# A fourth buffer for the q, k and v of a banded attention, and loads handed over six blocks ahead from the 16th block on

## The chip, the cores and the metric

The kernel runs on one core of a Trainium2 chip. The time is the device time of one execution in microseconds; less is better. The engines are TensorE (PE), VectorE (DVE), ScalarE (ACT), GpSimd (POOL) and SyncE (SP), which here only issues DMA transfers. Each engine works through a queue of its own in a fixed order and waits on semaphores for the others.

## What is computed

Three parts follow one another. The first is an attention in which each row sees itself and the 63 rows before it. The second adds the real part of a two-dimensional Fourier transform, and then an MLP on the normalised sum. The third is a gated MLP, whose mixing of rows is a product with a 576 by 576 matrix.

```
B, H, S, D = 4, 8, 576, 64                       # q, k, v
rel = pos[:, None] - pos[None, :]
scores = where((rel >= 0) & (rel < 64), q @ k.T / sqrt(D), -1e9)
x = softmax(scores) @ v                           # -> [B, S, 512]

mixed = real(fft(fft(x, axis=1), axis=2))
u = x + mixed
un = (u - mean(u)) / sqrt(var(u) + 1e-6)
x = u + maximum(un @ w_ch1, 0) @ w_ch2            # 512 -> 2048 -> 512

h = gelu(x @ w_in)                                # 512 -> 1024, in halves u, v
v = (v - mean(v)) / sqrt(var(v) + 1e-6) * g_ln
out = x + (u * (w_sg @ v + b_sg)) @ w_out
```

All is in float32. Where precision asks for it a number is split into a high and a low half, and one product becomes three matmuls (`mm3`, L130 to L132).

## The kernel before

**Attention.** The 4 x 9 = 36 blocks n have 64 query rows each. `scores` (L328) multiplies q by k for the eight heads, two heads at a time, into one of two PSUM tiles `sc`. VectorE adds the mask and finds the row's extreme (L333, results `s` and `mx`), and ScalarE takes the exponential (L335). One block later TensorE transposes the result into `pt` (L342), ScalarE copies it to `pts` (L344). Two blocks later, for two blocks at once, TensorE multiplies by v into the tile `pv` (L355), of which there is one in PSUM; VectorE normalises from there (L370 `rc`, L371 `rd`, L374 `x`). Three blocks later `x` is transposed (L384 `xt`) and copied to `uT` (L386), and VectorE folds it for the transform (L464 `E`, L465 `O`, L469, L470 `F`). In the last batch that is one fold over the whole batch, 128 x 1152, inside `dft`.

**Loads of attention.** All go over SP's queue. `load_q` fills one of `QB` tiles of a ring for two blocks, `load_k` one of three tiles for three blocks, `load_v` one of `VB` tiles for two blocks, with a lag of `VL` = 2 blocks. The loop hands over the loads of block n + 4 after the scores of block n. A load into a used tile waits until the last reader of the tile is done: `sc` for q and k, `pv` for v.

**What runs beside it.** `dft(b)` (L506 to L568) is the transform of batch b: first products with `eh` and `oh`, the halves of E and F, against a table (256 or 258 columns), then products with `ah`, `bh` against a second table (290 columns); VectorE adds the results into `uT` (L559 to L562). `ln(n)` is the layer norm of chunk n of 384 rows: transposes L637, statistics on VectorE (L641 BN_STATS, L642, L618 to L622, and `nb` at L648), ScalarE applies them (L650), then transposes L656 and copies L659, L661 into `xh` or `xhm`. LN(0) is the norm of the first chunk, LN(1) of the second. `raw` and `halves` decode weights: after a load `dec_s` three steps L166 (VectorE), L165 (ScalarE), L167 (VectorE) make a number, and L171 (ScalarE), L172 (VectorE in the MLP) split it into the tile `set`. In `mlp` TensorE makes `h` from `xh` and a set, ScalarE takes `rh` (L717), VectorE `rl` (L718), and TensorE multiplies these into four `acc` tiles; after the fourth set VectorE adds `acc` to `uT` (L703).

**What sets the order.** The parts are generators. A scheduler takes from them by their estimated times and priorities, and it fixes the order of every engine's queue when the kernel is built. The order of the instructions is nowhere written out: a wait that the estimate sees in one place moves what stands behind it on all engines. PSUM and SBUF tiles come from pools, and a tile of a pool is free for the next user when its last reader is done.

Of the kernel before, what the change touches and what calls it, by code (L numbers as in the profile page):

```python
# [11 lines left out]
F32 = mybir.dt.float32  # L12
# [33 lines left out]
LAG, XPT = (1, 2, 3), 0  # L46
STRETCH = (1.6, 1.0)
FP = ()
UB, SB, QB, VB = 4, 3, 3, 3
WARM, W0, W1 = 16, 9000, 2500  # L50
TAB_AT = (2, 4, 7, 9)
D45 = 3000
# [61 lines left out]
class Kernel:  # L114
# [152 lines left out]
        self.kt, self.vt = {}, {}  # L267

    def load_k(self, b, g):
        t = self.ap_.tile([128, 4, 256], F32, tag="k", bufs=3, name="k")  # L270
        o = 192 * g
        for c in (slice(0, 128), slice(128, 256)) if b == g == 0 else (slice(0, 256),):
            self.nc.sync.dma_start(t[:, :, c], self.aps["k"][b, :, :, o + c.start:o + c.stop])
            if b == g == c.start == 0:
                self.nc.scalar.dma_start(self.mask, self.aps["mask"])
        self.kt[b, g] = t
# [40 lines left out]
    def attention(self):  # L317
# [4 lines left out]
        def scores(n):  # L322
            b, j = divmod(n, NB)
            q, k = self.qt.pop((b, j)), self.kt[b, j // 3]
            sc = ps.tile([128, 4, 128], F32, tag="sc", bufs=2, name="sc")
            for hp in range(4):
                o = 64 * (j % 3)
                nc.tensor.matmul(sc[:, hp], lhsT=q[:, hp].rearrange("p a b -> p (a b)"), rhs=k[:, hp, o:o + 128], start=True, stop=True)  # L328
            mx = p.tile([128, 4], F32, tag="mx", bufs=3, name="mx")
            s = p.tile([128, 4, 128], F32, tag="s", bufs=SB, name="s")  # L330
            mask = self.mask[:, int(j == 0)]
            for hp in range(4):
                nc.vector.tensor_tensor_reduce(out=s[:, hp], in0=sc[:, hp], in1=mask, scale=-0.125, scalar=1e30, op0=ALU.add, op1=ALU.min, accum_out=mx[:, hp:hp + 1])  # L333
            for hp in range(4):
                nc.scalar.activation(out=s[:, hp], in_=s[:, hp], func=AF.Exp, bias=mx[:, hp:hp + 1], scale=-1.0)  # L335
            st[n], st['mx'] = s, mx

        def transposes(n):
            pr = st.pop(n)
            pt = ps.tile([128, 4, 128], F32, tag="pt", bufs=1 + XPT, name="pt")  # L340
            for hp in range(4):
                nc.tensor.transpose(pt[:, hp], pr[:, hp], self.ident)  # L342
            pts = p.tile([128, 4, 128], F32, tag="pts", bufs=3, name="pts")
            nc.scalar.activation(out=pts, in_=pt, func=AF.Copy)  # L344
            st[n] = pts

        def pv(n):

            b, j = divmod(n, NB)
            both = [n - 1, n] if j % 2 else [n]  # L350
            ops = [(64 * (m % NB % 2), st.pop(m), self.vt.pop((b, m % NB))) for m in both]
            st["pv"] = o = ps.tile([128, 2, 512], F32, tag="pv", name="pv")
            for i in range(8):
                for r, pts, v in ops:
                    nc.tensor.matmul(o[r:r + 64, i // 4, 65 * (i % 4):65 * (i % 4) + 65],  # L355
                                     lhsT=pts[:, i // 2, 64 * (i % 2):64 * (i % 2) + 64],
                                     rhs=v[:, 65 * i:65 * i + 65], start=True, stop=True)

        def norm(n):
            o = st["pv"]  # L360
            m = 64 if n % NB == NB - 1 else 128
            ov = o[:m, :, 0:260]
            if NV:
                y = p.tile([128, 2, 260], F32, tag="y", bufs=2, name="y")
                nc.scalar.activation(out=y[:m], in_=ov, func=AF.Copy)
                ov = y[:m]
            ov = ov.rearrange("p a (h e) -> p a h e", e=65)
            rc = p.tile([128, 2, 4, 1], F32, tag="rc", bufs=2, name="rc")
            rd = p.tile([128, 2, 4, 1], F32, tag="rd", bufs=2, name="rd")
            nc.vector.tensor_scalar(out=rc[:m], in0=ov[:, :, :, 64:65], scalar1=1e-9, scalar2=None, op0=ALU.add)  # L370
            nc.vector.reciprocal(out=rd[:m], in_=rc[:m])  # L371
            x = p.tile([128, 514], F32, tag="x", bufs=2, name="x")
            xv = x[:m].rearrange("p (a c) -> p a c", a=2)[:, :, 0:256].rearrange("p a (h e) -> p a h e", e=64)
            (nc.gpsimd if NV == 2 else nc.vector).tensor_tensor(out=xv, in0=ov[:, :, :, 0:64], in1=rd[:m].to_broadcast([m, 2, 4, 64]), op=ALU.mult)  # L374
            nc.gpsimd.tensor_scalar(out=x[:m, 256:257], in0=x[:m, 512:513], scalar1=1.0, scalar2=None, op0=ALU.mult)
            st["x", n] = x

        def xt(n):
            b, j = divmod(n, NB)
            m, x = 64 if j == NB - 1 else 128, st.pop(("x", n))  # L380
            i = j // 2
            t = ps.tile([128, 4, 128], F32, tag="pt", bufs=2, name="xt") if XPT else ps.tile([128, 4, 128], F32, tag="xt", name="xt")
            for c in range(4):
                nc.tensor.transpose(t[:, c, 0:m], x[:m, 128 * c:128 * c + 128], self.ident[:m, :m])  # L384
            t0 = S * b + 128 * i
            nc.scalar.activation(out=self.uT[:, :, t0:t0 + m], in_=t[:, :, 0:m], func=AF.Copy)  # L386
            self.folds(b, i, t)
            if j == NB - 1:
                self.xdone = b
# [8 lines left out]
        for n in range(N + LAG[2] + 1):  # L398
            if n in TAB_AT:
                tab_at = TAB_AT.index(n)  # L400
            else:
                tab_at = None
            if n < N:
                scores(n)
            if tab_at is not None:
                self.load_tables(tab_at, st["mx"])
            self.load_attn(n + 4)
            if n < N:
                yield 870
            m = n - LAG[0]  # L410
            if 0 <= m < N:
                transposes(m)
                yield 440
            m = n - LAG[1]
            if 0 <= m < N and full(m):
                pv(m)
                yield 1800 if m % NB % 2 else 900
                norm(m)
            m = n - LAG[2]
            if 0 <= m < N and full(m):  # L420
                xt(m)
                yield 440
# [1113 lines left out]
```

## Time and profile before

| | |
|---|---|
| median of 3 runs | 766.68 us (765.56 to 767.56) |
| the profiled execution | 765.43 us |
| its span, first to last instruction | 763.6 us |
| mean granted TensorE clock | 0.998 of full speed |
| PE busy | 746.0 us, 98% of the span |
| DVE busy | 526.7 us, 69% |
| ACT busy | 350.9 us, 46% |
| POOL busy | 192.6 us, 25% |
| bytes moved | 123.37 MB |

Busy is the time in which an engine works on an instruction. The profiled execution is one of several; the terms of a sum come from it, and its own time is to be held against the sum.

### The profile page before, as it was taken

What the parts mean: (1) busy time and instruction counts of PE and PEld (TensorE: products, weight loads), DVE (VectorE), ACT (ScalarE), POOL (GpSimd) and SP (SyncE); (2) the same over time, 40 slices, a digit from 0 to 9 for tenths busy, and PEclk for the clock granted to TensorE, in tenths of its full rate; (3) what the DMA queues carried; (4) which work ended last, traced back from release to release, by engine and by line L of the source; (5) the groups of instructions that cost most, each with busy time, mean ns of one, the idle gap of its engine ahead of it and who ended that gap; (6) DMA issues with size and microseconds to landing.
All of it is one profiled execution on the core that took longest, in us unless ns stands there. A gap on an engine that the chain in (4) does not pass through costs nothing.

```text
span 763.6 us, 13934 instructions
## 1 busy us (share of the span) xinstructions
PE 746.0 (98%) x4994; PEld 720.1 (94%) x4994; DVE 526.7 (69%) x1482; ACT 350.9 (46%) x837; POOL 192.6 (25%) x244
## 2 busy tenths in 40 slices
PE   7999899899999999999999999999999999999998
PEld 6798798899999999999999999999999898999897
DVE  4768857983446599874588658546987679674662
ACT  5896996745144566331245224124646454231220
POOL 2344464434214450065321112021102211010100
PEclk9999999999999999999999999999999999999999
DMA  9998761433016888584838914753111141114023
GB/s 267 320 298 258 202 209 43 140 110 125 1 30 215 281 262 292 190 330 161 319 118 318 355 59 151 289 207 124 57 58 32 40 132 33 63 32 135 11 73 124
DMA packets 84773, 123.37 MB, mean 162 GB/s; under 512 B 24416, under 2 KB 61664, under 8 KB 84704
## 3 DMA queue, kind: packets, MB, share of 16 engines
q1 hardware_dynamic: 82912, 119.13, 47.0%
q0 software_dynamic: 576, 2.97, 1.0%
q8 instruction: 39, 0.64, 0.3%
q10 hardware_dynamic: 1216, 0.39, 0.2%
q14 instruction: 30, 0.25, 0.1%
HBM read 91.79 MB, written 30.67 MB: 160 GB/s over the span
## 4 chain that ended last, share of the span: by engine, by line
PE 77%; DVE 3%; DMA 1%; issue 1%; ACT 0%; ACTq 0%
PE w L130 7%; PE w L132 7%; PE w L131 7%; PE c L132 6%; PE c L131 6%; PE c L130 6%; PE g L130 6%; PE g L132 6%; PE g L131 5%; PE acc L131 3%; PE acc L132 3%; PE h L130 3%; PE h L131 3%; PE h L132 3%; PE acc L130 3%; DMA dec_s<-in_wo 1%
## 5 line engine op out<-in xcount | busy, mean ns | idle before, releaser
L171 ACT ACTIVATE set<-dec_w 128x256 fp32r<-128x256 f32 x111 | 45.0, 414 | 68.8 <-PE w L131 31.1
L846 POOL TENSOR_TENSOR u<-u 128x384 f32<-128x384 f32 x15 | 18.6, 1243 | 184.8 <-ACT u L845 126.4
L619 POOL TENSOR_TENSOR rq<-rq,mhalf 128x1 f32<-128x1 f32 (+1 forms) x24 | 16.0, 665 | 150.8 <-DVE rq L618 149.7
L335 ACT ACTIVATE s<-s,mx 128x128 f32<-128x128 f32 x144 | 47.5, 393 | 13.3 <-DVE mx L333 13.2
L172 DVE TENSOR_TENSOR set<-dec_w,set 128x256 fp32r<-128x256 f32 x99 | 45.4, 467 | 9.7 <-ACT set L171 3.6
L333 DVE CUSTOM_DVE_ANT_0 s<-sc,mask 128x128 f32<-128x128 f32 x144 | 33.3, 284 | 24.7 <-PE sc L328 13.2
L165 ACT ACTIVATE dec_g<-dec_s 128x256 f32<-128x256 f32 x88 | 37.5, 428 | 27.4 <-DMA dec_s<-in_wi 11.5
L132 PE MATMUL acc<-rh,set 128*128 128x384 f32 x144 | 48.6, 338 | 0.0
L131 PE MATMUL acc<-rl,set 128*128 128x384 f32 x144 | 48.5, 337 | 0.0
L130 PE MATMUL acc<-rh,set 128*128 128x384 f32 x144 | 46.7, 337 | 0.0
L167 DVE SCALAR_TENSOR_TENSOR dec_w<-dec_g,dec_w 128x256 int32<-128x256 int32 x88 | 42.0, 480 | 3.2 <-ACT dec_g L165 2.9
L328 PE MATMUL sc<-k,q 128*128 128x128 f32 x288 | 40.2, 287 | 3.2 <-DVE mx L333 1.8
L846 DVE TENSOR_TENSOR u<-w,u 128x384 f32<-128x384 f32 x44 | 24.3, 552 | 27.4 <-POOL u L846 22.6
L328 PEld LDWEIGHTS sc<-k,q 128*128 128x128 f32 x288 | 35.8, 197 | 5.1 <-issue 1.8
L893 DVE TENSOR_TENSOR uT<-g,uT 128x384 f32<-128x384 f32 x36 | 19.3, 553 | 28.1 <-PE g L132 28.1
L130 PE MATMUL c<-set,set 128*128 128x320 f32 (+2 forms) x120 | 36.2, 303 | 0.0
L132 PE MATMUL c<-set,set 128*128 128x320 f32 (+2 forms) x120 | 36.0, 303 | 0.0
L718 DVE SCALAR_TENSOR_TENSOR rl<-h,rh 128x384 fp32r<-128x384 f32 x36 | 19.8, 551 | 23.3 <-ACT rh L717 23.3
L131 PE MATMUL c<-set,set 128*128 128x320 f32 (+2 forms) x117 | 35.1, 302 | 0.0
L166 DVE TENSOR_SCALAR dec_w<-dec_s 128x256 int32<-128x256 int32 x88 | 31.0, 361 | 5.0 <-DMA dec_s<-in_wo 3.5
L355 PEld LDWEIGHTS pv<-v,pts 128*64 128x64 f32 x576 | 23.3, 139 | 8.0 <-issue 6.4
L845 ACT ACTIVATE u<-w 128x384 f32<-128x384 f32 x29 | 14.1, 487 | 35.9 <-PE w L132 35.0
(383 smaller groups left out, 2603.2 us busy)
## 6 DMA issues: line engine op xcount, KB each, us to landing
dec_s<-in_w SPq DMA_DIRECT2D x64, 256.0 KB, 3.2
v<-in_v SPq DMA_DIRECT2D x16, 520.0 KB, 5.1
xht<-xb SPq DMA_DIRECT2D x10, 768.0 KB, 8.3
xhm<-xb SPq DMA_DIRECT2D x10, 768.0 KB, 7.6
xlm<-xb SPq DMA_DIRECT2D x8, 768.0 KB, 8.2
k<-in_k SPq DMA_DIRECT2D x11, 512.0 KB, 6.3
xf<-u SPq DMA_DIRECT2D x18, 256.0 KB, 3.1
p<-xf SPq DMA_DIRECT2D x24, 192.0 KB, 3.8
```

Of the source, the lines that this page charges most:

```text
L130: mm(out, lhsT=lh, rhs=rh, start=first and i == 0, stop=False)
L131: mm(out, lhsT=lh, rhs=rl, start=False, stop=False)
L132: mm(out, lhsT=ll, rhs=rh, start=False, stop=last and i == n - 1)
L165: nc.scalar.activation(out=g, in_=s[:, :, 1].bitcast(F32), func=AF.Prelu, scale=2.0 ** -112, alpha=-2.0 ** 32)
L166: nc.vector.tensor_scalar(out=w, in0=s[:, :, 0], scalar1=29, scalar2=None, op0=ALU.logical_shift_right)
L167: nc.vector.scalar_tensor_tensor(out=w, in0=g[:].bitcast(I32), scalar=3, in1=w, op0=ALU.logical_shift_left, op1=ALU.bitwise_or)
L171: self.nc.scalar.activation(out=hi, in_=f, func=AF.Copy)
L172: self.low.tensor_tensor(out=lo, in0=f, in1=hi, op=ALU.subtract)
L328: nc.tensor.matmul(sc[:, hp], lhsT=q[:, hp].rearrange("p a b -> p (a b)"), rhs=k[:, hp, o:o + 128], start=True, stop=True)
L333: nc.vector.tensor_tensor_reduce(out=s[:, hp], in0=sc[:, hp], in1=mask, scale=-0.125, scalar=1e30, op0=ALU.add, op1=ALU.min, accum_out=mx[ ...
L335: nc.scalar.activation(out=s[:, hp], in_=s[:, hp], func=AF.Exp, bias=mx[:, hp:hp + 1], scale=-1.0)
L846: add = lambda eng, o, i, j: eng.tensor_tensor(out=o, in0=i, in1=j, op=ALU.add)
```

## The change

The ring of q gets a fourth tile, and so do the pools of k and v. The loop hands over the loads of block n + 4 for the first 16 blocks, at block 16 those of blocks 20, 21 and 22 together, and from then on those of block n + 6.

```diff
-UB, SB, QB, VB = 4, 3, 3, 3
+UB, SB, QB, VB, KB = 4, 3, 4, 4, 4
+FAR = 16
...
-        t = self.ap_.tile([128, 4, 256], F32, tag="k", bufs=3, name="k")
+        t = self.ap_.tile([128, 4, 256], F32, tag="k", bufs=KB, name="k")
...
-            self.load_attn(n + 4)
+            for m in {True: (n + 4,), n == FAR: (n + 4, n + 5, n + 6), n > FAR: (n + 6,)}[True]:
+                self.load_attn(m)
```

The number of matmuls and of transfers stays as it is. Two memsets each come to VectorE and GpSimd for the fourth q tile (L264, L265). Since the scheduler sees other loads, the order on all engines is another one from about the ninth block on, until some 200 us; behind that the same instructions follow in the same order, but for the numbers of some tiles. In the changed text all lines behind the new one are one further down, and behind the new loop two, so that L641 of before is L643, L656 is L658, and L166 is L167.

VectorE at the statistics of LN(0), among the blocks of attention. Before, two BN_STATS (L641) and a decode step (L166) stand around `rc`, and a second decode step stands right ahead of `x` some rows further down:

```order
L641 BN_STATS st<-u 128x6 x2
L642 BN_AGGR mv<-st 128x2
L370 TENSOR_SCALAR rc<-pv 128x8
L166 TENSOR_SCALAR dec_w<-dec_s 128x256
L642 BN_AGGR mv<-st 128x2
L371 RECIPROCAL rd<-rc 128x8
```

In the changed order, the same place, one BN_STATS and one fold of attention stand there; behind the last row come four reductions and `x`, and a decode step follows behind it:

```order
L643 BN_STATS st<-u 128x6
L644 BN_AGGR mv<-st 128x2
L371 TENSOR_SCALAR rc<-pv 128x8
L466 TENSOR_TENSOR E<-xt,uT 128x2x128
L467 TENSOR_TENSOR O<-xt,uT 128x2x128
L644 BN_AGGR mv<-st 128x2
L372 RECIPROCAL rd<-rc 128x8
```

The decode steps have moved from ahead of `x` to behind it.

TensorE at the same place. Before, between two products `pv`, the second of which needs `x` to be done with the first:

```order
L355 MATMUL pv<-v,pts 64x65 x16
L342 MATMUL pt<-ident,s 128x128 x2
L384 MATMUL xt<-ident,x 128x128 x2
L342 MATMUL pt<-ident,s 128x128 x2
L328 MATMUL sc<-k,q_104 128x128 x4
L355 MATMUL pv<-v,pts 64x65
```

In the changed order:

```order
L356 MATMUL pv<-v,pts 64x65 x16
L639 MATMUL g<-ident,uT 128x128
L385 MATMUL xt<-ident,x 128x128 x2
L329 MATMUL sc<-k,q_107 128x128
L343 MATMUL pt<-ident,s 128x128 x4
L329 MATMUL sc<-k,q_107 128x128 x3
L639 MATMUL g<-ident,uT 128x128 x5
L356 MATMUL pv<-v,pts 64x65
```

Six transposes of LN(0) (L639) have come between the two.

VectorE at the hand-over from attention to the MLP. Before, `nb` of LN(1) stands ahead of the large folds of the last batch and ahead of the decode steps of the MLP's next weights:

```order
L622 SCALAR_TENSOR_TENSOR rs<-rq_2428,rq_2426 128x3
L648 SCALAR_TENSOR_TENSOR nb<-mv,rs 128x3
L464 TENSOR_TENSOR E<-uT 128x1152
L465 TENSOR_TENSOR O<-uT 128x1152
L166 TENSOR_SCALAR dec_w<-dec_s 128x256 x2
L469 TENSOR_TENSOR E<-E 128x2x288
```

In the changed order the folds come first, and the last rows ahead of `nb` are these (L705 is the sum `uT<-acc`, L173 the low half of a weight):

```order
L173 TENSOR_TENSOR set_2192<-dec_w,set_2192 128x256
L624 SCALAR_TENSOR_TENSOR rs<-rq_2433,rq_2431 128x3
L168 SCALAR_TENSOR_TENSOR dec_w<-dec_g,dec_w 128x256
L167 TENSOR_SCALAR dec_w<-dec_s 128x256
L705 TENSOR_TENSOR uT<-acc,uT 128x384 x2
L167 TENSOR_SCALAR dec_w<-dec_s 128x256
L650 SCALAR_TENSOR_TENSOR nb<-mv,rs 128x3
```

From the fold `E` (128 x 1152) to `nb` these are 62 instructions: among them 14 of L167, 12 of L168, 10 of L173, three `rl` and the two sums.

TensorE at the transposes L656 (L658) of LN(1), which need `u` and with it `nb`. Before, they come among the products of the second weight set of chunk 0:

```order
L132 MATMUL h<-xh_119,set_70 128x384
L130 MATMUL h<-xh_119,set_70 128x384
L131 MATMUL h<-xl_120,set_70 128x384
L656 MATMUL g<-ident,u 128x128
L130 MATMUL g<-tab,oh 128x256
```

In the changed order they come behind the last product of the fourth set into `acc`:

```order
L133 MATMUL acc<-rh_2201,set_2190 128x384
L132 MATMUL acc<-rl_2202,set_2190 128x384
L133 MATMUL acc<-rh_2201,set_2190 128x384
L658 MATMUL g<-ident,u 128x128
L131 MATMUL g<-tab,oh 128x256
```

From the products with `ah` of two rows, the last of dft(1), to the first L658 TensorE has 97 matmuls of 384 columns, 29 of 256 to 290 columns and 12 transposes.

## Rows read from the trace of the kernel before

**Rows 1.** Stretches: length; busy (count) PE, PEld, DVE, ACT, POOL; PEclk; DMA share; GB/s.

```profile
0.00:160.00 160.00, 147.91 (x1474) 134.57 (x1475) 119.84 (x519) 124.16 (x334) 70.66 (x118) 0.99 0.74 220
160.00:763.60 603.60, 598.08 (x3522) 585.51 (x3520) 406.91 (x964) 226.76 (x504) 121.96 (x126) 1.00 0.42 146
...
80.00:90.00 10.00, 7.91 (x92) 6.89 (x90) 9.19 (x43) 9.52 (x28) 7.49 (x11) 0.83 0.69 197
...
130.00:140.00 10.00, 9.23 (x70) 8.39 (x69) 8.66 (x18) 7.34 (x16) 4.80 (x9) 1.00 0.15 44
140.00:150.00 10.00, 8.56 (x55) 8.21 (x56) 9.96 (x19) 6.96 (x20) 5.70 (x5) 1.00 0.56 174
```

**Rows 2.** What TensorE waited for in 0 to 160 us: total, times, longest.

```profile
PE pv L355 <- issue: 2.1, 1, 2.1
...
PE h L130 <- DVE rl L718: 1.4, 1, 1.4
PE sc L328 <- DMA k<-in_k: 1.3, 2, 1.2
...
PE g L656 <- ACT u L659: 0.6, 1, 0.6
```

**Rows 3.** Timeline of TensorE, 12 and 82 to 87 us: start, length, instruction, idle before.

```profile
12.30 0.91 PE L328 MATMUL sc<-k,q 128*128 128x128 f32 x6 [1.16 <-DMA k<-in_k]
...
82.09 1.06 PE L328 MATMUL sc<-k,q 128*128 128x128 f32 x8
85.23 0.30 PE L355 MATMUL pv<-v,pts 128*64 128x65 f32 x2 [2.09 <-issue]
85.46 2.00 PE L328 MATMUL sc<-k,q 128*128 128x128 f32 x8
```

**Rows 4.** Timeline of GpSimd (first row) and VectorE, 80 to 87 us.

```profile
81.75 1.31 POOL L483 TENSOR_TENSOR el<-E,eh 128x578 fp32r<-128x578 f32 x1 [0.83 <-ACT eh L482]
...
80.73 1.27 DVE L641 BATCH_NORM_STATS2 st<-u 128x6 f32<-128x512 f32 x2
82.01 0.12 DVE L370 TENSOR_SCALAR rc<-pv 128x8 f32<-128x8 f32 x1
82.06 1.16 DVE L166 TENSOR_SCALAR dec_w<-dec_s 128x256 int32<-128x256 int32 x1
...
83.91 0.63 DVE L166 TENSOR_SCALAR dec_w<-dec_s 128x256 int32<-128x256 int32 x1
84.45 0.68 DVE L374 TENSOR_TENSOR x<-pv,rd 128x512 f32<-128x512 f32 x1
...
86.46 0.41 DVE L464 TENSOR_TENSOR E<-xt,uT 128x256 f32<-128x256 f32 x1
```

**Rows 5.** Busy time by stretches, as rows 1, behind the wait of place A.

```profile
85.25:89.00 3.75, 3.75 (x28) 3.35 (x30) 2.97 (x17) 3.27 (x10) 2.50 (x5) 0.54 0.45 158
```

**Rows 6.** DMA issues: queue, count, KB each, median us to landing.

```profile
k<-in_k SPq DMA_DIRECT2D x11, 512.0 KB, 6.3
```

**Rows 7.** Timeline of VectorE and ScalarE, 133 to 148 us.

```profile
133.19 0.16 DVE L648 SCALAR_TENSOR_TENSOR nb<-mv,rs 128x3 f32<-128x3 f32 x1
133.94 1.79 DVE L464 TENSOR_TENSOR E<-uT 128x1152 f32<-128x1152 f32 x1 [0.58 <-ACT uT L386]
135.66 1.35 DVE L465 TENSOR_TENSOR O<-uT 128x1152 f32<-128x1152 f32 x1
...
146.58 0.42 DVE L172 TENSOR_TENSOR set<-dec_w,set 128x256 fp32r<-128x256 f32 x1
...
147.45 1.51 DVE L172 TENSOR_TENSOR set<-dec_w,set 128x256 fp32r<-128x256 f32 x1
...
133.81 2.22 ACT L650 ACTIVATE u<-u,nb,rs 128x512 f32<-128x512 f32 x3
```

**Rows 8.** Timeline of TensorE, first matmul of MLP chunk 0, then transposes L656.

```profile
133.11 0.44 PE L130 MATMUL h<-xh,set 128*128 128x384 f32 x1
...
137.21 0.27 PE L656 MATMUL g<-ident,u 128*128 128x128 f32 x1
...
139.96 0.66 PE L656 MATMUL g<-ident,u 128*128 128x128 f32 x4 [0.56 <-ACT u L659]
```

## The prediction

> **What bounds the kernel now.** Read the busy time by stretches first, then what TensorE waited for, and last the timeline of the two places where it waits. TensorE is busy for 147.91 of the first 160 us and for 598.08 of the 603.60 behind them [rows 1]: whatever the change does can only touch the 17.6 us in which it is not, 12.1 before 160 us and 5.5 behind. So attention, the transform stage that is woven into it, and the hand-over to the MLP hold two thirds of all that can be won, and the change works just there. Two places stand out: 80 to 90 us, where TensorE is busy for 7.91 of 10 us and its granted clock is 0.83, and 140 to 150 us with 8.56 [rows 1].
>
> TensorE's waits before 160 us have names [rows 2]. The longest is one wait of 2.1 us at a PV product, the next 1.4 us at an MLP matmul for `rl`. For a load of q, k or v it waits 1.3 us in all, twice, both on `k` [rows 2], and 1.16 of that are at 12.30 [rows 3]. **No load of attention is late from the 16th block on**: `k`, the largest of the three per block, lands 6.3 us after its issue [rows 6], and no wait names a load there. What the change alters for the clock on the wall must therefore come from the order that it makes, not from the loads.
>
> **Place A, 83 to 85 us.** TensorE ends its score products and stands until 85.23 [rows 3]. The page puts that down to "issue", since a wait for several semaphores is shown by the last. The matmul writes the one `pv` tile in PSUM, and that tile is free when VectorE has read it (`x<-pv,rd`): VectorE begins that at 84.45, and it ends at 85.13 [rows 4], 0.10 before TensorE starts. VectorE was late because between `rc` and `x` its queue held two decode steps and, ahead of `rc`, two BN_STATS of LN(0): 1.27 us for these, 1.16 and 0.63 us for the decode steps [rows 4]. Behind that wait the granted clock falls: 0.54 over 85.25 to 89 us, so mostly at the 1.2 GHz level instead of 2.4 [rows 5]; eight score products take 2.00 us instead of the 1.06 of their sisters ahead of the wait [rows 3]. Of 3.75 us, 46% are lost: **1.7 us** beside the wait of 2.09.
>
> **The change, part by part.** *The fourth q tile* adds two memsets on VectorE and two on GpSimd in the first 4 us. VectorE has nothing to do before its first scores, and TensorE's first products wait for `k`: nothing, and at the most some tenths. *The fourth k and v tiles* issue no instruction. *Handing over six blocks ahead* moves the same loads on SP's queue; their number and size are the same. With three buffers the load of block n+4 already waits for the buffer's reader; with four buffers and n+6 it waits for the same reader, so transfers land about as early, seen from their use, as before. Price: 0.
>
> *The order.* Everything else is in what the scheduler makes of it, from about the ninth block on. At place A TensorE's rows show, between the two blocks of `pv`, four `pt`, two `xt` and four `sc` before, and six transposes L639 more in the changed order; four such transposes take 0.66 [rows 8], so that is 0.7 to 1.0 us more cover, and 0.7 since they overlap. VectorE's rows show, between `rc` and `x`, no decode step in the changed order. The two took 1.79 of the 2.44 us from `rc` (82.01) to `x` (84.45); in their place stand the two folds `E` and `O`, 0.41 each, and one reduction more [rows 4]: some 0.7 less. One of the BN_STATS is no longer right ahead, another 0.6 if its wait counts. By the one and the other the 2.09 us fall to somewhere from 0 to 0.8. The next longest wait, 1.44 in 140 to 150 us, left the clock at 1.00 [rows 1, 2], so the 1.7 us go as well. Gain 3.0 to 3.8 us; I take 3.6.
>
> What the Trainium skill says of the long decode step: its page "SBUF — State Buffer" (the part on engine and DMA sides) has one port pair shared by VectorE and GpSimd as a lock held for a whole instruction, the later one fully blocked. The trace agrees: the decode step of 1.16 us runs beside GpSimd's `el`, 81.75 to 83.06 [rows 4]. By it a decode step at another place is either short or waits out a GpSimd instruction, so VectorE's time at place B would be its low end plus GpSimd's time there, 5.70 us in 140 to 150 [rows 1]: 26.3, close to the middle of my two ends.
>
> *Place B, the hand-over.* Here the new order looks worse. Before, VectorE had the statistics of LN(1) done with `nb` at 133.19, ahead of the large folds of dft(3) (`E` at 133.94) and of the MLP's decode steps [rows 7]; TensorE reached the L656 transposes at 137.21 and did not wait [rows 8]. In the changed order `nb` is the 62nd VectorE instruction counted from `E`: 14 steps L166, 12 L167, 10 L172, three `rl`, and two sums `uT<-acc` stand ahead of it. On TensorE the L656 transposes come behind all four weight blocks of MLP chunk 0.
>
> What VectorE needs for these 62: the decode steps from 146.58 to 147.45 follow at 0.29 us each (three in 0.87) [rows 7]; 62 of them, with 2.6 us more for the two large folds (1.79 and 1.35 less two steps), are 20.6 us. The other end is the pace of the whole stretch of before, 37 instructions in 18.6 busy us of 130 to 150 [rows 1], 0.50 each: 31 us. `E` stands behind a copy of ACT and two VectorE instructions after the last large product of dft(1), 1.5 us at that pace, and ACT's L650 behind `nb` takes 0.74 (three in 2.22 [rows 7]): `u` is ready 22.8 to 33.2 us behind that product. TensorE's work in the same stretch: 97 matmuls of 384 columns at 0.178 (23 of them from 133.11 to 137.21 [rows 8]), 17.3 us, and 29 of 256 to 290 columns and 12 transposes at some 0.13 (by the columns, and by the 0.66 for four), together 5.3: 22.6. Idle time in the stretch is 0.2 to 10.6. One chain sets a floor: the two `uT<-acc` of chunk 0 need TensorE's last product of it, and it is the last work ahead of L656; behind it stand `uT<-acc` twice, a decode step and `nb`, 1.2 to 2.0 us, and L650, less the TensorE work that is left when the first sum may start: about 1.5 us. The middle of 1.5 and 10.6 is 6.0; I take **6.2**, a little towards the pace of 0.50, which is the row nearest to this work. Before, the same waits were 1.44 and 0.56 [rows 2], 2.0 in all. Place B costs 4.2 us.
>
> Sum: 763.6 - 3.6 + 4.2 = 764.2 of span, which is 0.6 more, or 766.0 for an execution like the profiled one (765.43). That execution is 1.25 below the median of the runs, so the forecast beside that median is 766.68 + 0.6 = **767.3**. Less than 0.3%, 2.3 us, is about what a measurement of this kernel cannot tell from nothing.
>
> **The rivals.** *Faster: the wait at A goes and B costs little.* It needs VectorE near 0.29 us per step, so that only the floor of 1.5 to 3 us is left at B. For it: VectorE is busy for 119.84 of the first 160 us [rows 1]; a new order may use some of its idle 40 to have the decode done sooner than I count. Against: 9.96 busy of 10 in 140 to 150. Result: -0.5 to +1.0 at B, with -3.8 at A: 762.4 to 763.9. Chance 0.30.
>
> *Slower: LN(1) becomes late by the contended pace.* `nb` at the 0.50 end, idle 8 to 10.6 at B; a wait longer than the 2.09 of place A also drops the clock, 1.7 more. It decides when the pace is above some 0.42 us. -3.6 + 6 to 8.6 + 1.7 is 770.8 to 773.4; without the clock from 769.1; with A left standing and B as taken 770.9. For it: the count of instructions ahead of `nb` on an engine without slack. Against: at that very pace the order of before kept TensorE waiting only 2.0 us. Chance 0.34.
>
> *The loads matter after all.* If loads from block 16 on were what attention waits for, six blocks of lead would bring them in earlier. Against: 1.3 us of load waits in all, nearly all of it ahead of block 4 [rows 2, 3]. It would give no more than the forecast without place B, 763; I count it with the faster case. The page "DMA: Bandwidth & Descriptors" of the Trainium skill (Rules for kernel authors) says to issue a transfer early and wait for it late; here that is done already.
>
> *Nothing comes of it* (both places stay): 766.7, part of the middle case.
>
> **How the numbers follow.** The likeliest case is the sum, A gained and B given back, anywhere within 2.3 us of no change: 0.36, 764.4 to 769.0, and 767.3 is its sum. Faster 0.30 (762.4 to 764.4), slower 0.34 (769 to 773.4). The range leaves out the last part of the slower case, a tenth, and takes in a little below the faster one: 762.0 to 771.8.
>
> **What would show it.** Right at A: no wait of 2 us at a PV product near 83 us, and a granted clock of 1.00 in each slice from 70 to 120 us. Right at B: TensorE waits for ACT's `u` at the L656 transposes (L658 in the changed text), 4 us or more, with VectorE busy without a gap ahead of it and `nb` behind the decode steps; and a wait for `rl` of 1 to 3 us ahead of it. The loads: no `k`, `q` or `v` among TensorE's waits behind 13 us, as before. Wrong if the clock falls at another place, if SP's longer queue of loads holds back the decode's transfers (VectorE would wait for `dec_s`), or if LN(0), which now crosses later blocks, stalls there.

## The result: slower by 1.3%

The changed kernel takes 775.60 us (773.66 to 777.23, five runs), the kernel before on the same chip 765.64 (763.87 to 767.56, five runs). The ratio is 1.0130, with a 95% interval of 1.0114 to 1.0145: 10 us slower. The forecast was 767.3, and 771.8 was the end of its range.

The profiled execution of the changed kernel is the slowest of its five: 777.23 us, span 775.4, mean granted clock 0.988 (before 765.43, 763.6, 0.998). Its stretches, with the columns of [rows 1]:

```profile
0.00:160.00 160.00, 142.31 (x1415) 128.96 (x1415) 113.69 (x522) 116.47 (x316) 65.85 (x113) 0.97 0.78 210
160.00:775.40 615.40, 609.55 (x3579) 595.58 (x3579) 408.23 (x963) 236.42 (x522) 128.93 (x133) 0.99 0.42 146
80.00:90.00 10.00, 10.00 (x130) 9.15 (x130) 8.99 (x46) 8.76 (x24) 6.84 (x9) 1.00 0.69 187
```

TensorE stands still for 17.69 of the first 160 us, against 12.1 in [rows 1], and place A is gone: 80 to 90 us is full, at clock 1.00, where 7.91 of 10 stood at 0.83. So the loss lies elsewhere. What TensorE waited for in the first 160 us, total, times and longest, to be held against [rows 2]:

```profile
PE sc L329 <- DMA k<-in_k: 3.0, 3, 1.6
PE pv L356 <- DMA v<-in_v: 2.9, 1, 2.9
...
PE sc L329 <- DMA q<-in_q: 1.8, 1, 1.8
```

The waits for loads are now 7.7 us; before they were 1.3. TensorE's timeline (start, duration, what; in brackets the idle time ahead and who ended it) shows where, and the largest wait of the whole kernel just behind 160 us:

```profile
9.18 1.13 PE L329 MATMUL sc<-k,q 128*128 128x128 f32 x8 [1.80 <-DMA q<-in_q]
13.30 0.91 PE L329 MATMUL sc<-k,q 128*128 128x128 f32 x6 [1.60 <-DMA k<-in_k]
29.82 3.29 PE L329 MATMUL sc<-k,q 128*128 128x128 f32 x16 [1.09 <-DMA k<-in_k]
44.01 0.45 PE L356 MATMUL pv<-v,pts 128*64 128x65 f32 x2 [2.89 <-DMA v<-in_v]
...
160.54 0.48 PE L658 MATMUL g<-ident,u 128*128 128x128 f32 x1 [4.00 <-ACT u L652]
```

Finer stretches, first of before, then of after:

```profile
0.00:15.00 15.00, 10.47 (x66) 9.55 (x67) 5.36 (x38) 6.74 (x18) 4.04 (x18) 1.00 0.91 237
15.00:30.00 15.00, 13.89 (x189) 12.05 (x190) 10.44 (x59) 12.71 (x37) 3.82 (x10) 1.00 1.12 363
30.00:50.00 20.00, 19.28 (x220) 17.34 (x217) 15.52 (x90) 16.39 (x49) 10.18 (x19) 1.00 1.02 307
...
70.00:100.00 30.00, 26.50 (x291) 23.65 (x290) 25.46 (x120) 26.06 (x70) 12.93 (x21) 0.94 0.73 205
100.00:130.00 30.00, 29.97 (x328) 26.66 (x326) 20.58 (x86) 22.84 (x60) 16.58 (x24) 1.00 0.43 137
130.00:170.00 40.00, 37.79 (x249) 36.48 (x249) 36.08 (x75) 24.30 (x59) 16.71 (x19) 1.00 0.39 119
```

```profile
0.00:15.00 15.00, 9.19 (x58) 8.28 (x58) 4.97 (x32) 5.81 (x15) 4.56 (x20) 1.00 0.93 208
15.00:30.00 15.00, 13.12 (x169) 11.61 (x168) 10.10 (x62) 11.70 (x33) 2.38 (x8) 1.00 1.15 314
30.00:50.00 20.00, 16.33 (x149) 14.51 (x149) 11.78 (x57) 11.22 (x31) 7.30 (x14) 0.76 1.12 290
...
70.00:100.00 30.00, 29.87 (x351) 27.22 (x348) 28.29 (x151) 27.52 (x78) 13.78 (x20) 1.00 0.74 216
100.00:130.00 30.00, 28.15 (x312) 24.65 (x310) 17.94 (x86) 26.54 (x71) 17.43 (x26) 1.00 0.52 169
130.00:170.00 40.00, 34.72 (x217) 31.86 (x216) 31.05 (x75) 25.50 (x59) 18.76 (x19) 0.91 0.35 108
```

Read each as time lost: length less busy PE, and on top length times what the clock lacks of 1.00. The difference after less before:

| stretch | idle | clock | together |
|---|---|---|---|
| 0 to 50 us | 5.0 | 4.8 | +9.8 |
| 70 to 100, with place A | -3.4 | -1.8 | -5.2 |
| 100 to 130 | 1.8 | 0 | +1.8 |
| 130 to 170, with place B | 3.1 | 3.6 | +6.7 |

With +0.4 for 50 to 70 and -0.6 behind 170 the sum is 12.9; the span grew by 11.8. It is a reading, not exact: the same work stands up to 12 us later, and a stretch's clock has two digits. It is also the reading of one execution, the slowest: `bufs_only`, which has the same order and the same tiles (see below) and was profiled at 774.55 us, lost 4.8 us idle and 1.8 by the clock in its first 50. The prediction has terms for the second and the fourth row; the first is not in it.

Also to be seen: in the first 15 us DMA is as busy as before (0.93 and 0.91) and moves 208 GB/s instead of 237. The median from issue to landing of `k` is 7.7 us where [rows 6] show 6.3.

### The profile page after: what moved, and what is told of

It reads as the page before. It is cut to its first block, busy times and chain, and to the rows that moved or that the text cites. A ratio compares the mean times of both kernels' runs of the same rounds, so it can differ in the third digit from the quotient of the medians.

```text
span 775.4 us, 13952 instructions
## 1 busy us (share of the span) xinstructions
PE 751.9 (97%) x4994; PEld 724.5 (93%) x4994; DVE 521.9 (67%) x1484; ACT 352.9 (46%) x837; POOL 194.8 (25%) x246
## 4 chain that ended last, share of the span: by engine, by line
PE 88%; DVE 5%; DMA 4%; issue 1%; ACT 1%; SPq 0%; DVEq 0%; ACTq 0%
PE w L131 7%; PE w L133 7%; PE w L132 7%; PE g L131 7%; PE g L133 6%; PE g L132 6%; PE c L133 6%; PE c L131 6%; PE c L132 6%; PE sc L329 3%; DMA k<-in_k 3%; PE h L133 3%; PE h L132 3%; PE h L131 3%; PE acc L131 3%; PE acc L133 3%
## 5 line engine op out<-in xcount | busy, mean ns | idle before, releaser
L173 DVE TENSOR_TENSOR set<-dec_w,set 128x256 fp32r<-128x256 f32 x99 | 44.3, 455 | 9.5 <-PE h L132 3.3
L166 ACT ACTIVATE dec_g<-dec_s 128x256 f32<-128x256 f32 x88 | 37.5, 429 | 24.2 <-DMA dec_s<-in_wi 10.1
L329 PE MATMUL sc<-k,q 128*128 128x128 f32 x288 | 41.8, 293 | 6.4 <-DMA k<-in_k 3.0
L329 PEld LDWEIGHTS sc<-k,q 128*128 128x128 f32 x288 | 37.6, 204 | 8.4 <-issue 3.9
L168 DVE SCALAR_TENSOR_TENSOR dec_w<-dec_g,dec_w 128x256 int32<-128x256 int32 x88 | 40.8, 466 | 2.7 <-ACT dec_g L166 2.4
L167 DVE TENSOR_SCALAR dec_w<-dec_s 128x256 int32<-128x256 int32 x88 | 28.7, 333 | 4.9 <-DMA dec_s<-in_wo 3.0
L719 ACT ACTIVATE rh<-h 128x384 fp32r<-128x384 f32 x36 | 17.5, 485 | 31.8 <-PE h L133 31.7
```

Source lines behind the costliest of these rows:

```text
L166: nc.scalar.activation(out=g, in_=s[:, :, 1].bitcast(F32), func=AF.Prelu, scale=2.0 ** -112, alpha=-2.0 ** 32)
L167: nc.vector.tensor_scalar(out=w, in0=s[:, :, 0], scalar1=29, scalar2=None, op0=ALU.logical_shift_right)
L168: nc.vector.scalar_tensor_tensor(out=w, in0=g[:].bitcast(I32), scalar=3, in1=w, op0=ALU.logical_shift_left, op1=ALU.bitwise_or)
L173: self.low.tensor_tensor(out=lo, in0=f, in1=hi, op=ALU.subtract)
```

## Experiments

Each ratio is to the kernel before, run on the same chip. The diffs start from the changed kernel unless said.

**Buffers without the far hand-over, and each fourth buffer by itself.** `bufs_only` keeps four buffers and always hands over block n + 4; `q4` and `kv4` have some of the four.

```diff
-FAR = 16
+FAR = 999                            # bufs_only
-UB, SB, QB, VB, KB = 4, 3, 4, 4, 4
+UB, SB, QB, VB, KB = 4, 3, 4, 3, 3   # q4, with FAR = 999
+UB, SB, QB, VB, KB = 4, 3, 3, 4, 4   # kv4, with FAR = 999
```

> Four buffers each for q, k and v, but every block hands over the loads of block n + 4 as before. The kernel as it is built has the same rows in the same order on TensorE and VectorE as the changed kernel. Theory 1 (the fourth buffers make the order, the distance of the hand-over does nothing): 775 us, with the same waits for q, k and v in the first 50 us. Rival (the loads handed over six ahead crowd the queue): back near 766 us.

> Only q gets the fourth buffer, hand-over at n + 4. SP's queue then has q for two more blocks ahead of k and v that are needed sooner, much as in the changed kernel. Theory 1 (q that runs ahead in a full transfer system makes k and v late; the order that follows from it also puts nb of LN(1) behind the folds): 773 to 777 us, TensorE idle 10 us or more in the first 50 us and the clock below 0.95 there. Rival (where the tiles lie in SBUF slows the transfers): about a third of the loss, 768 to 770.

> Only k and v get the fourth buffer, hand-over at n + 4. q goes out as before; v and k move ahead of decode loads only, and nb stays ahead of the large folds. Theory 1: no loss in the first 50 us (idle about 6 us, as before), 764 to 768 us. Rival (placement in SBUF, two thirds of the added bytes): 770 to 773 us.

`bufs_only`: 775.54 us, 1.0135 (1.0120 to 1.0150), the whole loss. All its queues have the same instructions in the same order as the changed kernel's: with four buffers the far hand-over alters nothing. `q4`: 766.42, 1.0013 (0.9997 to 1.0029), no change that can be told from noise: place A shrinks to 0.57 us there, and the longest wait at L658 is 1.1. `kv4`: 770.03, 1.0062 (1.0045 to 1.0079). The loss is that of several buffers together.

**The q loads in their old tiles at first.** The first nine q loads go round three of the four tiles.

```diff
-        t, o = self.qring[(b * 5 + j // 2) % QB], j % 2
+        m = b * 5 + j // 2
+        t, o = self.qring[m % 3 if m < 9 else (m - 6) % 4], j % 2
```

> Four buffers each and the hand-over of the changed kernel, but the first nine loads of q go round three of the tiles only; the fourth is used from the tenth on. The early queue of SP has q where it was before, and nb of LN(1) stands ahead of the large folds. Theory 1: both losses go, 762 to 767 us. Rival (placement in SBUF, or simply more buffers): the early loss of some 10 us stays, 770 us or more.

771.67 us, 1.0085 (1.0054 to 1.0115). A third of the loss went, and yet DMA moves 210 GB/s in the first 15 us, as in `bufs_only` (211) and `kv4` (210), though q goes round four tiles from the start in one of the three alone. What they share is an address: one v tile is 2 x 520 floats per partition, 4160 bytes, 8 times 512 and 64. A fourth one moves other tiles of the same pool in SBUF, those of mask, q and k among them, from starts at multiples of 512 to starts 64 bytes off.

**The starts alone.** In `after_on_line` the x tile is 56 floats wider; two of them are 448 bytes, with the 64 a whole 512. In `before_off_64` and `before_off_256`, made from the kernel before, x is 522 and 546 wide, and the starts are off by 64 and by 256 bytes. The order stays as it was in each.

```diff
-            x = p.tile([128, 514], F32, tag="x", bufs=2, name="x")
-            xv = x[:m].rearrange(...
+            x = p.tile([128, 570], F32, tag="x", bufs=2, name="x")
+            xv = x[:m, 0:514].rearrange(...
```

> The changed kernel, but each of two x tiles is 224 bytes wider, so that the pool of attention begins 448 bytes lower and mask, q and k start at multiples of 512 bytes again, as before (the fourth v tile of 4160 bytes had put them at 448 past such a multiple, 192 past one of 256). Order on TensorE and VectorE row by row that of the changed kernel. Theory 2 (the starts of the tiles slow the transfers): the loss of the first 50 us goes, DMA in 0 to 15 us back at 235 GB/s, 766 to 769 us, what is left being the wait for LN(1). Theory 1 (the order of the loads makes them late): 775 us as it was.

> The kernel before, but each of two x tiles is 32 bytes wider, so that mask, q and k start 448 bytes past a multiple of 512, where the changed kernel has them. Order row by row that of before. Theory 2: 5 to 10 us slower, 770 to 776 us, DMA near 210 GB/s in 0 to 15 us and waits for q and k in the first 45 us. Theory 1: 765.6 us, as before.

> As the last one, but 128 bytes wider each, so that mask, q and k start 256 past a multiple of 512. Theory 2 with a boundary of 256 bytes: 765.6 us, as before. With a boundary of 512 bytes: slower by as much as the one before this. Theory 1: 765.6 us.

`after_on_line`: 772.63 us, 1.0097 (1.0081 to 1.0113), 2.5 us less than the changed kernel by the two ratios. `before_off_64`: 767.59, 1.0029 (1.0016 to 1.0041): the kernel before loses 2.2 us by its addresses alone. `before_off_256`: 765.09, 0.9998 (0.9986 to 1.0011): nothing. The first 15 us of the three, in this sequence:

```profile
0.00:15.00 15.00, 10.30 (x58) 9.27 (x58) 5.08 (x33) 6.19 (x15) 4.55 (x20) 0.91 0.91 241
```

```profile
0.00:15.00 15.00, 9.96 (x68) 9.20 (x69) 5.36 (x38) 7.00 (x19) 4.04 (x18) 1.00 0.96 223
```

```profile
0.00:15.00 15.00, 10.92 (x69) 10.15 (x70) 5.36 (x38) 7.04 (x19) 4.04 (x18) 1.00 0.91 244
```

The last columns, share and GB/s, tell it: with the 64 bytes DMA is busier and moves less. The Trainium skill, "DMA: Bandwidth & Descriptors" (How a descriptor splits into AXI transactions), has a transfer cut into transactions that must start at multiples of 256 bytes, with extra beats where the transfer does not start at one. It says so of what is read; the side that moved here is the one written, in SBUF, of which it says nothing. The two runs show the same pattern on that side: 64 off costs, 256 off does not.

**The same correction for two of the others.**

> The kernel with four buffers whose first nine loads of q go round three tiles, with the same wider x tiles, so that q and k start at multiples of 512 bytes. nb of LN(1) stands ahead of the large folds in its order. Theory 2: some 6 us less than without the wider tiles, 764 to 767 us. Theory 1: 771.7 us as it was.

> Only k and v get the fourth buffer, hand-over at n + 4, and wider x tiles put q and k at multiples of 512 bytes. Theory 2 (starts of the tiles): 2 to 4 us of the 4.4 that this kernel lost without go, 766 to 768 us. If the order of the loads of k and v costs the rest: 770 us.

`q_late_on_line`: 768.26, 1.0040 (1.0026 to 1.0054), against 1.0085. `kv4_on_line`: 767.04, 1.0019 (1.0009 to 1.0029), against 1.0062. So the starts are worth 2.2 to 3.4 us in all four orders in which they were tried. With starts as before, a fourth k and v cost 1.5 us, a fourth q nothing, the three together 7.4.

**Place B: decode ahead of the statistics.** `low_17_24` gives VectorE's low halves of eight decode pieces to GpSimd, on top of `after_on_line`; `b_low_17_24` does so in the kernel before. `no_stats` leaves out the statistics of LN(1) (its mean is taken as 0 and its scale as 1), again on `after_on_line`.

```diff
-        self.low.tensor_tensor(out=lo, in0=f, in1=hi, op=ALU.subtract)
+        low = self.nc.gpsimd if 17 <= self.ndec <= 24 else self.low
+        low.tensor_tensor(out=lo, in0=f, in1=hi, op=ALU.subtract)
...
-            V.bn_stats(out=st[:r], in_=u[:r])
+            if n != 1:
+                V.bn_stats(out=st[:r], in_=u[:r])
...
+        if n == 1:
+            nc.gpsimd.memset(rs, 1.0)
+            nc.gpsimd.memset(nb, 0.0)
```

> The changed kernel with q and k at multiples of 512 bytes (wider x tiles), and the low halves of eight weight pieces (two sets of the MLP) made on GpSimd instead of VectorE, which is the decode work that stood between the statistics and nb of LN(1). Order on VectorE as in the changed kernel up to there; nb comes 14 rows earlier and ahead of the sums uT<-acc. Theory B (nb behind decode steps costs the wait of 4.0 us and the clock behind it): the wait at the L658 transposes falls below 2 us, the granted clock in 130 to 170 us is 1.00 instead of 0.91, 765 to 768 us against 772.6 without. Rival (the loss behind the starts of the tiles is early, in the first 50 us, from the order of the loads): 771 us or more.

> The kernel before with the same eight low halves on GpSimd: the control for the last one. nb of LN(1) was ahead of this work already, so theory B expects no more than the 1.4 us that TensorE waits for rl to change: 764 to 766 us. If GpSimd relieves VectorE all over, it gains as much as the last one did, 3 us or more.

> The changed kernel with wider x tiles, and the statistics of LN(1) left out: its mean and scale are constants from memsets, so that the transposes of LN(1) wait for no VectorE step. Theory B (nb behind decode steps): the wait of 4.0 us at the transposes falls below 1 us and the granted clock in 130 to 170 us is 1.00, 765 to 768 us. Rival (TensorE has run out of other work there and waits for what is next, ScalarE's copies and xhm): the idle of 130 to 170 us stays at 4 us or more, 770 to 773 us.

`low_17_24`: 770.52, 1.0075 (1.0055 to 1.0095), beside 1.0097; the intervals overlap, so the run does not tell theory B from its rival. The wait for `u` at the same transposes splits into one of 2.11 and one of 1.44 us instead of going. `b_low_17_24`: 765.48, 0.9992 (0.9982 to 1.0003), nothing. `no_stats`: 765.90, 0.9999 (0.9987 to 1.0011). Without VectorE's chain, and with TensorE's order another one from about 143 us on, there is no wait at L658, and its stretch is that of before:

```profile
130.00:170.00 40.00, 37.71 (x241) 35.42 (x241) 31.14 (x68) 25.41 (x63) 18.43 (x18) 1.00 0.38 119
```

against 37.79 busy at 1.00 before and 34.72 at 0.91 in `after_on_line`. Against 772.63 us for that kernel the statistics cost it 6.7 us by the two times, and 7.5 by the two ratios (1.0097 and 0.9999).

**The early wait for v.** The profiled execution of `after_on_line` (769.23) is the fastest of its runs and has no wait for `v`, so the same kernel was run and profiled once more.

> The same kernel as the changed one with wider x tiles, profiled once more, since the execution profiled first was the fastest of its five, by 3 us. If the 3 us are a load of v that comes late in most executions: a wait for v of 2 to 3 us near 41 us in this profile, 771 to 773 us. If not: no such wait.

That execution took 772.70 us and has the wait. Rows of its timeline and stretches:

```profile
32.97 1.13 PE L329 MATMUL sc<-k,q 128*128 128x128 f32 x8 [1.75 <-DMA q<-in_q]
34.47 1.15 PE L356 MATMUL pv<-v,pts 128*64 128x65 f32 x16
...
40.06 0.45 PE L356 MATMUL pv<-v,pts 128*64 128x65 f32 x2 [2.53 <-DMA v<-in_v]
```

```profile
0.00:15.00 15.00, 10.42 (x72) 9.52 (x74) 6.20 (x43) 7.37 (x19) 4.54 (x20) 1.00 0.91 249
15.00:30.00 15.00, 14.21 (x181) 12.80 (x180) 10.88 (x72) 11.73 (x34) 3.06 (x10) 1.00 1.13 348
30.00:50.00 20.00, 15.72 (x158) 14.39 (x157) 12.04 (x56) 12.88 (x37) 7.46 (x14) 0.83 0.99 318
...
70.00:100.00 30.00, 29.31 (x333) 26.19 (x332) 28.43 (x154) 27.70 (x76) 14.82 (x23) 1.00 0.71 207
130.00:170.00 40.00, 34.77 (x204) 32.60 (x203) 29.39 (x72) 24.83 (x57) 18.47 (x17) 0.91 0.36 119
```

The first 30 us are those of before again. In 30 to 50 us it loses 3.6 us idle and 3.4 by the clock against before. It is the load of the first v tile of the second batch that is late. SyncE's rows of the changed kernel (start, time that it stays at these issues) show what it is handed over behind, on a DMA with no free share:

```profile
24.76 2.88 SPq L285 DMA_DIRECT2D q<-in_q  x2
27.68 3.96 SPq L274 DMA_DIRECT2D k<-in_k  x2
31.73 2.75 SPq L302 DMA_DIRECT2D v<-in_v  x1
```

In `v_first` each block's hand-over has its load of v ahead of those of q and k, `low_v_first` has that and `low_17_24`.

```diff
+        if VL <= n < B * NB + VL:
+            b, j = divmod(n - VL, NB)
+            if j % 2 == 0:
+                self.load_v(b, j)
```

(the same four lines go out behind the loads of q and k)

> The changed kernel with wider x tiles, and in each block's hand-over the load of v ahead of those of q and k. nb of LN(1) stays behind decode steps. Theory (order of the loads: v comes late behind q and k that ran ahead): no wait for v, 769 to 770.5 us against 772.6. Rival (DMA is full, and which load stands first only moves the wait): 772 us or more, the wait then being for q or k.

> The last one, and the low halves of eight weight pieces on GpSimd, as run before without v first (770.5 us). If the three losses (starts of the tiles, v behind q and k, decode ahead of nb) are apart from each other, the gain at place A is what is left: 764 to 768 us. If they are not, 769 us or more.

`v_first`: 771.87, 1.0088 (1.0064 to 1.0111), with a wait of 2.78 us for `v` at 39.78. It does not test the order of the loads: in SP's queue, as the scheduler made it, that load of v stands behind 13 issues of q and 7 of k, just as in the changed kernel. `low_v_first`: 773.76, 1.0108 (1.0088 to 1.0128); the gains of the two edits don't add up, and each makes a new order.

Two things that the traces show bear on this wait. First, the load takes long: from issue to landing 12.1 us in `on_line_again` (27.85 to about 39.9) and in the changed kernel, 13.7 in `v_first`, and 4.6 before (32.90 to 37.5). `bufs_only`, with the changed kernel's order, has the wait too. The profile puts it down to a fold `E`, which the product does not read; the load, issued at 31.57, landed 12.4 us later, at 44.0:

```profile
44.14 0.30 PE L356 MATMUL pv<-v,pts 128*64 128x65 f32 x2 [1.45 <-DVE E L471]
```

Second, the changed order asks for the tile sooner. Before, these are the last product with v of the first batch (one block, x16) and the first of the second batch:

```profile
33.11 1.15 PE L355 MATMUL pv<-v,pts 128*64 128x65 f32 x16
...
40.59 1.15 PE L355 MATMUL pv<-v,pts 128*64 128x65 f32 x32
```

They begin 7.5 us apart, with 48 matmuls between them. In `on_line_again` the second is ready to begin at 37.53, where its wait starts, 3.1 us behind the first, with 16 matmuls between. A load that lands at 39.9 would have been in time for the product of before, at 40.59, and one that lands at 37.5 for the changed order's. In the first profile of `after_on_line` the load landed at 37.9, and the product began at 37.98 without a wait.

**The far hand-over on three buffers.** Here a load may overwrite a q tile whose last products come later in program order, so some scores are taken with the q of later blocks: these products can wait for a load that is none of theirs.

```diff
-UB, SB, QB, VB, KB = 4, 3, 4, 4, 4
+UB, SB, QB, VB, KB = 4, 3, 3, 3, 3
```

> The hand-over of the change alone: three buffers each, loads of n + 6 from block 16 on. Tiles start where they did before. The order differs from that of before only behind some 45 us (LN(0) comes earlier, nb of LN(1) stays ahead of the folds). Theory: no load is late either way, no loss in the first 50 us and none at the hand-over to the MLP: 763 to 768 us.

771.81, 1.0078 (1.0065 to 1.0092); its largest wait, 4.56 us, is one for `rl` at the MLP. As a test of the far hand-over by itself it decides nothing, for the reason just given.

**Which buffer brings the wait for v.** Both with starts as before and block n + 4 throughout.

```diff
+UB, SB, QB, VB, KB = 4, 3, 4, 3, 4   # qk4_on_line, x left at 514
+UB, SB, QB, VB, KB = 4, 3, 4, 4, 3   # qv4_on_line, x at 570
```

> q and k with a fourth buffer, v with three, loads always four blocks ahead; the pools keep the starts that they had before. In the order as built the k of one tile further on still goes ahead of the first v tile of the second batch, as in the changed kernel, and the statistics of LN(1) stand ahead of the large folds, as in the kernel before. Theory K (the fourth k tile lets a k transfer go ahead of that v, and DMA is full, so v comes late): TensorE waits 2 us or more for v between 38 and 45 us and its clock falls behind it, 769 to 771, ratio 1.004 to 1.007. Rival P (the fourth v tile is what matters, since with it the scheduler takes the PV product of that tile earlier): no wait of over 1 us for v there, 765.5 to 768, ratio 1.000 to 1.003.

> q and v with a fourth buffer, k with three, loads always four blocks ahead; starts as before. The k that went ahead of the first v tile of the second batch now goes behind it; the statistics of LN(1) stand behind the large folds, as in the changed kernel, so the wait of some 4 us at the hand-over stays. Theory K: no wait of over 1 us for v between 38 and 45 us, 768.5 to 770.5, ratio 1.004 to 1.0065. Rival P: TensorE still waits 2 us or more for v there, 771.5 to 774, ratio 1.008 to 1.011.

`qk4_on_line`: 774.44 us, 1.0127 (1.0105 to 1.0149). `qv4_on_line`: 771.04, 1.0086 (1.0067 to 1.0105). TensorE's timeline of the first:

```profile
36.43 1.15 PE L356 MATMUL pv<-v,pts 128*64 128x65 f32 x16 [1.57 <-DMA v<-in_v]
...
47.31 1.15 PE L356 MATMUL pv<-v,pts 128*64 128x65 f32 x32
...
90.07 0.30 PE L356 MATMUL pv<-v,pts 128*64 128x65 f32 x2 [1.99 <-issue]
...
150.65 0.44 PE L131 MATMUL h<-xh,set 128*128 128x384 f32 x1 [4.67 <-DVE rl L720]
```

and of the second:

```profile
32.83 1.13 PE L329 MATMUL sc<-k,q 128*128 128x128 f32 x8 [1.44 <-DMA q<-in_q]
39.10 0.30 PE L356 MATMUL pv<-v,pts 128*64 128x65 f32 x2 [1.71 <-DMA v<-in_v]
```

Neither time lies where either theory put it, but the two waits are not for the same tile. In `qk4_on_line` the one of 1.57 us is at the last product of the first batch (x16), whose load there stands behind two of k; the first tile of the second batch comes without a wait, at 47.31, with 58 matmuls between. In `qv4_on_line` that tile is waited for, 1.71 us, with 16 matmuls between, although the second k now goes behind it. That speaks against theory K and for rival P as far as this wait goes. The fourth v tile is not enough for it, since `kv4_on_line` has no such wait. And `qk4_on_line` is as slow as the changed kernel, and by other waits: one of the kind of place A, at 90.07, stands again, and the MLP's wait for `rl`, 1.44 before [rows 2], is 4.67.

## Why the prediction was wrong

**The step that failed** is *Handing over six blocks ahead*, with the fourth k and v tiles beside it: "transfers land about as early, seen from their use, as before. Price: 0." Stretches 0 to 50 us cost 9.8 us in the profiled execution (6.6 in that of `bufs_only`), of which no part was in the sum. The sign that the prediction gave itself, no load among TensorE's waits behind 13 us, failed at 29.82 and 44.01. Two causes are shown, one of them only in part.

The first is the address. That a fourth tile "issues no instruction" is right, and it was taken for "costs nothing": a fourth v tile of 4160 bytes moves its neighbours off the multiples of 256 bytes. It costs 2.2 us in the order of before (`before_off_64`) and 2.5 in the new one (`after_on_line`). It comes on top where DMA has no slack: in the first 50 us the median of v from issue to landing is 8.6 us in `before_off_64` and 7.5 before (k 6.9 and 6.7), and DMA's share is 0.91 to 1.12 in the first 50 us of before, and the sum made no use of that column.

The second is the new order in the first 50 us, which was taken as ending in place A alone. With starts as before the three buffers lose 7.4 us; 6.7 of them are place B and -4.6 place A (`on_line_again`, 70 to 100: 2.8 idle and 1.8 clock), so about 5.3 are left for the rest. That is a sum and not an experiment of its own; the windows of `on_line_again` give 6.7 for 0 to 50 us (3.3 idle, 3.4 by the clock) and 1.4 for 100 to 130. Most of it are the waits for `q` and `v` between 30 and 40 us, 1.75 and 2.53, with the clock behind them.

The wait for the first v tile of the second batch is shown in eight traces: the changed kernel, `bufs_only` (1.45 us), `on_line_again`, `no_stats` (2.56), `low_17_24` (2.83), `v_first`, `low_v_first` (1.95) and `qv4_on_line`. In all eight TensorE's order has 8 or 16 matmuls between the last product with v of the first batch and this one; only the first profile of `after_on_line` has that order and no wait. The eleven other traces, before and `q4`, `kv4_on_line` and `qk4_on_line` among them, have 47 to 58 matmuls there, and none waits for this tile. So the likely cause is both together, an order that asks for the tile sooner and a load that lands later. No run moves the product or the load alone, so this is read from the traces and not shown by an experiment.

**Place A** held, mechanism and place: no wait at the PV product, clock 1.00 from 70 to 100 us. Foreseen was a gain of 3.6 us, measured are 5.2 by the windows, for the wider stretch; the next one, 100 to 130, loses 1.8 more than before. Of the gain the 1.7 by the clock are less sure than the wait: `before_off_64` has the order of before and the same wait, 2.11 us, and its clock stays at 1.00 from 70 to 100 us.

**Place B** held as mechanism and was sized too small: 4.2 foreseen, 6.7 by the windows and 6.7 to 7.5 by `no_stats`. VectorE's rows end as the order said, with `nb` behind the decode:

```profile
134.25 1.82 DVE L466 TENSOR_TENSOR E<-uT 128x1152 f32<-128x1152 f32 x1
...
158.37 1.00 DVE L705 TENSOR_TENSOR uT<-acc,uT 128x384 f32<-128x384 f32 x2
159.30 0.27 DVE L167 TENSOR_SCALAR dec_w<-dec_s 128x256 int32<-128x256 int32 x1
159.50 0.14 DVE L650 SCALAR_TENSOR_TENSOR nb<-mv,rs 128x3 f32<-128x3 f32 x1
```

```profile
134.25:159.50 25.25, 21.50 (x133) 20.46 (x130) 25.25 (x63) 14.99 (x38) 11.26 (x10) 1.00 0.40 124
```

From `E` to `nb` it is 25.25 us, with VectorE (third busy column) busy in all of it, between the ends of 20.6 and 31. The 6.2 us that were taken stand for 26.6 (22.6 and 6.2, less 1.5 and 0.74), so the size of VectorE's part was about right. The Trainium skill's rule of the shared port ("SBUF — State Buffer") had given 26.3, close as well, but in part by luck: the 5.70 in that sum is GpSimd's time in ten microseconds of before, and in these 25.25 us GpSimd was busy for 11.26 (fifth busy column), by which the same sum gives 31.9. One decode step of 1.02 us at 151.82, beside GpSimd's `grow` at 150.88 to 152.57, looks like the rule. Idle time was thus no more than foreseen: 5.3 in 130 to 170, with 4.00 in one piece; the wait for `rl`, foreseen as 1 to 3 us, was 0.6. What was missing is the clock. It was put with the slower rival only; here it is

```profile
161.00:166.00 5.00, 4.89 (x25) 4.52 (x23) 0.24 (x1) 4.27 (x9) 1.98 (x3) 0.50 0.20 53
```

half, the level of 1.2 GHz, for 5 us behind the wait, and 3.6 us lost in 130 to 170. The likeliest case already had a wait of 6.2 us; place A, with 2.09, had shown that a shorter one can lower it.

**The rivals.** *Slower* came true for its clock, not for its pace: 0.41 us per instruction (25.25 by 62), below the 0.42 from which it was to decide. *The loads matter after all* came true with the sign turned: what matters is not when they are handed over but at what rate they move and, as far as the traces tell, how soon TensorE's order asks for them. The fourth q tile's memsets cost nothing that can be told from noise (`q4`).

No version beat the kernel before; the nearest with any of the new buffers is `q4`.

## What to carry over

A buffer that issues nothing still has a size: where that is no multiple of 256 bytes it can move the starts of other tiles, as here, and the start of each tile that DMA fills is worth a look before and after. Where a scheduler makes the order, a change to pools is a change to all of it: here five sets of buffers, with starts as before, gave ratios of 1.001 to 1.013, by waits in different places, so cost the first fifty microseconds and their DMA share as closely as the stalls that one hopes to remove. Put the clock behind a wait in the likeliest case, not in a rival, once a row shows a shorter wait that lowers it, and give it a chance of its own, since the same wait lowers it in one run and not in another. Before a run is read as a test of the order of loads, look whether the queue as built has them in another order at all.

## What the runs showed of the chip

A start 64 bytes off, on the same loads in the same order, took DMA from 237 to 223 GB/s in the first 15 us and the kernel from 1.000 to 1.0029; 256 bytes off cost nothing. In the changed kernel a wait of 2.89 us for `v`, with TensorE busy for 0.12 of the 3 us ahead of 44 us, was followed by six microseconds at half clock:

```profile
44.00:50.00 6.00, 5.99 (x49) 5.31 (x50) 1.86 (x7) 1.96 (x5) 2.95 (x6) 0.50 1.05 284
```

so that wait cost 2.9 us by itself and 3 by what came behind it. What comes behind a wait is not the same each time. The wait at place A, in one and the same order, lowered the granted clock of 70 to 100 us to 0.94 before (2.09 us) and in `before_off_256` (2.10), and left it at 1.00 in `before_off_64`:

```profile
87.36 0.30 PE L355 MATMUL pv<-v,pts 128*64 128x65 f32 x2 [2.11 <-issue]
```

The 4.0 us at L658 were followed by a clock of 0.91 over 130 to 170 us in the changed kernel, and of 0.96 in `v_first`.
